# Late weight loads held on other filter rows, and the second batch's first stage started two steps later: a study of one change to a fused FFT-mixing and feed-forward kernel

## The chip, the cores and the metric

The kernel runs on one core of one Trainium2 chip. The metric is device time in microseconds (us) for one execution of the whole program.

A profile is one execution, recorded by the hardware. PE is TensorE (matmuls), PEld its weight loads, DVE is VectorE, ACT is ScalarE, POOL is GpSimd, SP is SyncE, which here only issues DMA transfers. "SPq" marks such an issue. Times in the profile count from the start of the span.

## The reference

Two stages, 8 batches of 3008 tokens of width 256.

```python
X = np.fft.rfft(x, axis=1)                       # x: (8, 3008, 256)
Y = X * (filt_r + 1j * filt_i)[None, :, :]       # filters: (1505, 256)
y = np.fft.irfft(Y, n=3008, axis=1)
h = y.reshape(-1, 256) @ w_in                    # w_in: (256, 2048)
g = h * (1 / (1 + np.exp(-beta * h)))
out = g @ w_out                                  # w_out: (2048, 256)
```

## The kernel before

The FFT is done as matmuls with small tables, in stages. Batch 0 is transformed first (about 35 us). Then the feed-forward part runs as 752 block steps, 16 to a block of 512 tokens, and the stages of the next batches are spread over these steps by a plan: `place(a, z, units)` spreads `units` over the steps `a` to `z`. One step is two matmuls of 512 columns with `win` (line 825), ACT's activation `gT`, and four matmuls of 256 columns with `wout` two steps later (line 860). All of it is in program order on each engine, so a unit of another batch that waits in PE's queue stops the block steps behind it: in the profile of before, step 2's matmuls stand behind a unit of line 619 that waited 1.75 us and start at 39.24 us.

The parts that matter here, cut:

```python
apool = pool("apool", 3)                     # three buffers for tiles with the tag "a1"
# ...
def load_filter(f_sb, filt, at, k0, n, eng): # "lo" rows: at..at+H; "hi" rows: at+H..at+M  (H = 32, M = 64)
    # ... returns [issue of the lo rows, issue of the hi rows]
for part in FG[1:]:                          # filter groups 1, 2, 3, on SyncE
    for h in (1, 0):                         # hi rows are issued first, then lo rows
        for f, at in ((filt_r, 0), (filt_i, M)):
            load_filter(fri, f, at, *part, nc.sync)[h]()
# ...
# The hold: GpSimd copies one element of a filter load, so it waits until that load has landed
# before it issues what stands behind in its own queue (profile of before: the hold ends at
# 23.1 us, the first win load is issued at 23.42 us).
held = setup.tile([P, 1], F32, name="held", tag="held")
for p0 in (0, M):
    gp.tensor_copy(held[p0 : p0 + H], fri[p0 : p0 + H, 3 * KG - 1, :1])
load_win(0); load_win(1); load_wout(0)
xs[1] = load_x(1, X_HALVES[:2])              # first half of batch 1's x
# ... some microseconds later, during batch 0's middle stages:
for h in range(1, 4):
    load_wout(h)
load_x(1, X_HALVES[2:], xs[1])               # second half of batch 1's x
mark3 = dpool.tile([1, D], BF16, name="mark3", tag="mark3")
nc.sync.dma_start(mark3[:], xs[1][:1, J - 1, :])   # a tiny transfer: holds SyncE until that half has landed (46.2 us)
# ... and behind it, still on SyncE:
for at in (0, M):
    for go in load_filter(frr, filt_r, at, 0, JG, nc.sync):   # four loads of 256 KB
        go()
zz0[0] = apool.tile([KP, JG, D], BF16, name="zz", tag="a1")   # batch 0 takes one of the three buffers
# ...
def s1(b, i, on_act):                        # stage 1: 16 units, a buffer "a1" for every 4 of them
    if jj == 0:
        s["a1"] = apool.tile([KP, JG, D], BF16, name="a1", tag="a1")
    ps = fpsum.tile([P, 512], F32, name="ps1", tag="f")
    nc.tensor.matmul(ps[:KP], lhsT=t1[:], rhs=s["x"][:, 2 * i : 2 * i + 2, :], start=True, stop=True)   # line 619
    evac(s["a1"][:, jj : jj + 2, :], ps[:KP], on_act)
    if jj + 2 == JG:
        nc.sync.dma_start(s["d1r"][:, g * JG : (g + 1) * JG, :], s["a1"][:])   # line 624: out to DRAM
# ...
    units = u1(1, True)                      # stage 1 of batch 1
    place(1, 7, units[: J // 4], per=2)
    at = place(9, 14, units[J // 4 :], per=2)
```

Of the kernel before, what the change touches and what calls it, by code (L numbers as in the profile page):

```python
# [24 lines left out]
M = 64  # L25
H = M // 2
NK = 24
J = 32
# [9 lines left out]
def kernel(  # L38
# [364 lines left out]


    held = setup.tile([P, 1], F32, name="held", tag="held")
    for p0 in (0, M):
        gp.tensor_copy(held[p0 : p0 + H], fri[p0 : p0 + H, 3 * KG - 1, :1])
    def load_win(h):
        fs = slice(h * FF // 2, (h + 1) * FF // 2)
# [216 lines left out]
    def a2_read(b):  # L626
        s = st[b]
        s["a2"] = []
        for h in range(NG):
            t = a2pool.tile([P, KG, D], BF16, name="a2", tag="a2")  # L630
            nc.sync.dma_start(t[:], s["d1c"][:, h * KG : (h + 1) * KG, :])
            s["a2"].append(t)
# [41 lines left out]
    def zz_read(b):  # L674
        s = st[b]
        s["zz"] = []
        for h in range(NJG):
            t = zzpool.tile([KP, JG, D], BF16, name="zz", tag="zz")
            nc.sync.dma_start(t[:], s["d2r"][:, h * JG : (h + 1) * JG, :])
            s["zz"].append(t)  # L680
# [15 lines left out]
    def place(a, z, units, clear=False, per=1):  # L696
        last_at = a
        for n, go in enumerate(units):
            at = a + (z - a) * n / max(1, len(units) - 1)
            at = max(int(at), last_at)  # L700
            if clear and (at % NFB < 2 or at % NFB > 13):
                at += (2 - at) % NFB
            while len(plan.get(at, ())) >= per:
                at += 1
            plan.setdefault(at, []).append(go)
            last_at = at
        return last_at

    def u1(b, act=False):
        def unit(i):  # L710
            def go():
                if i == 0:
                    start(b)
                s1(b, i, act and i % 2 == 1)

            return go

        return [unit(i) for i in range(J // 2)]

    def u23(b):  # L720
        return [lambda i=i: s23(b, i) for i in range(NK // 2 + VLAG)]

    def u4(b, act=False):
        return [lambda i=i: s4(b, i, act and i % 2 == 1) for i in range(J // 2)]
# [6 lines left out]
    def uf():  # L731
        return [
            go
            for k0 in range(JG, NK, JG)
            for at in (0, M)
            for go in load_filter(frr, filt_r, at, k0, JG, nc.sync)
        ]


    def ut(n):  # L740
        return [
            lambda k=k: nc.vector.tensor_scalar_mul(
                t3[M:P, k : k + NK // n], t3b[M:P, k : k + NK // n], -1.0
            )
            for k in range(0, NK, NK // n)
        ]
# [11 lines left out]
    first_step = [(S * b // TB) * NFB for b in range(B + 1)]  # L758
    if B > 1:
        units = u1(1, True)  # L760
        place(1, 7, units[: J // 4], per=2)
        at = place(9, 14, units[J // 4 :], per=2)
        place(at + 1, at + 1, [lambda: a2_read(1)] + uf(), per=9)
        place(14, 20, ut(4), per=2)
        at = place(25, 56, u23(1), per=2)
        assert at < 60
        place(60, 60, [lambda: zz_read(1)], per=9)
        place(67, 79, u4(1), per=2)
# [43 lines left out]
    for s in range(len(steps) + LAG):  # L812
# [28 lines left out]
        if s >= LAG:  # L841
# [16 lines left out]
            per = acc[0].shape[1]  # L858
# [48 lines left out]
```

## Time and profile before

792.9 us (median of 3 runs, 792.88 to 793.45). The profiled execution took 790.78 us, and its span is 788.9 us.

| quantity (profile of before) | value |
|---|---|
| PE busy | 777.6 us of 788.9 (99%) |
| largest PE wait on a DMA up to 100 us | 1.75 us, first half of batch 1's x |
| hold ends; first win load issued | 23.1 us; 23.4 us |
| second half of batch 1's x lets SyncE go on | 46.2 us |
| first stage-1 write issued | 48.3 us |

The head of the page gives the span and, for each engine, its busy time, share of the span and number of instructions.

```profile
span 788.9 us, 15550 instructions
...
PE 777.6 (99%) x6111; PEld 548.4 (70%) x6111; DVE 394.4 (50%) x645; ACT 597.0 (76%) x922; POOL 144.7 (18%) x143
```

PE is busy for 99%, so time can be won only where it idles or where its clock is reduced. The list of waits up to 100 us (engine, output and line, what it waited for; total us, times, longest) has these lines among others.

```profile
DVE a L109 <- DMA d<-a: 2.2, 1, 2.2
...
PE ps L619 <- DMA xg<-in_x_dram: 1.8, 1, 1.8
...
```

The second line is PE's wait for x.

PE's timeline around the wait (start, duration, engine, line, operation, output and inputs, shapes, count; in brackets the idle time before and what ended it):

```profile
35.87 1.03 PE L825 MATMUL hps<-y,win_sb 128*128 128x376 bf16 x6
38.66 0.78 PE L619 MATMUL ps<-xg,t 94*96 94x512 bf16 x2 [1.75 <-DMA xg<-in_x_dram]
39.24 1.06 PE L825 MATMUL hps<-y,win_sb 128*128 128x512 bf16 x2
```

The stages' table for the same time: stretch, its length, busy time of PE, PEld, DVE, ACT, POOL with the number of instructions, then the granted PE clock, the DMA engines' mean share and GB/s.

```profile
22.00:24.00 2.00, 1.68 (x24) 1.46 (x23) 2.00 (x6) 2.00 (x5) 1.17 (x3) 1.00 0.84 197
24.00:26.00 2.00, 2.00 (x34) 1.91 (x32) 2.00 (x4) 2.00 (x5) 2.00 (x4) 1.00 0.49 49
36.00:38.00 2.00, 0.91 (x6) 0.32 (x4) 0.37 (x2) 1.73 (x4) 0.86 (x1) 1.00 0.99 246
38.00:40.00 2.00, 1.34 (x4) 0.61 (x5) 0.69 (x1) 0.52 (x1) 0.00 (x0) 0.75 1.00 352
40.00:42.00 2.00, 2.00 (x13) 1.44 (x12) 0.75 (x2) 0.76 (x2) 1.47 (x1) 0.50 1.18 317
42.00:44.00 2.00, 2.00 (x14) 1.28 (x13) 0.54 (x1) 1.04 (x2) 2.00 (x2) 0.89 1.01 215
```

From 36 to 40 us PE is not full, and from 39 to 42.4 us its clock is granted at half (0.50 in the trace's record of the clock, for 3.413 us). At 24 to 26 us the DMA engines are half idle (share 0.49). GpSimd's timeline tells why: nothing is issued while it waits for the filter rows (3.79 and 0.34 us).

```profile
22.19 0.41 POOL L407 COPY held<-fri 32x1 f32<-32x1 f32 x1 [3.79 <-DMA fri<-in_filt_r_dram]
22.94 0.18 POOL L407 COPY held<-fri 32x1 f32<-32x1 f32 x1 [0.34 <-DMA fri<-in_filt_i_dram]
23.42 1.54 POOL L410 DMA_DIRECT2D win_sb<-in_moe_w_in_dram  x2 [0.30 <-issue]
```

SyncE's timeline shows when the second half of x has landed (the tiny transfer `mark<-xg` is issued in that moment), four filter loads behind it, and then the first stage-1 write. (That half comes in two transfers. The tiny one reads from the larger, which landed at 46.20 us; the smaller landed at 46.77 us.)

```profile
46.21 0.23 SPq L506 DMA_DIRECT2D mark<-xg  x1
46.48 0.31 SPq L131 DMA_DIRECT2D frr<-in_filt_r_dram  x1
...
48.33 6.05 SPq L624 DMA_DIRECT2D d<-a  x3
...
```

### The profile page before, as it was taken

Reading aid. Unit: us, or ns where it says so; the run is one execution under the profiler, and the core shown is the slowest. Engines: PE = TensorE matmul, PEld = TensorE weight load, DVE = VectorE, ACT = ScalarE, POOL = GpSimd, SP = SyncE. Lnnn points to the kernel's source line nnn. Section 1 sums busy time; section 2 is a strip of 40 time slices with the busy share of each in tenths; the row PEclk is TensorE's granted clock in tenths of the full one; section 3 lists DMA queues with packets and bytes.
Section 4 is the critical chain, followed back from the end, with each engine's and each line's share of the span. In section 5 each row is a group of like instructions: output and inputs, shape, how many; then the busy total and the mean of one; then the engine's idle time right before and its main releaser. Section 6 shows DMA issues by size and latency. Waiting matters only on the chain.

```text
span 788.9 us, 15550 instructions
## 1 busy us (share of the span) xinstructions
PE 777.6 (99%) x6111; PEld 548.4 (70%) x6111; DVE 394.4 (50%) x645; ACT 597.0 (76%) x922; POOL 144.7 (18%) x143
## 2 busy tenths in 40 slices
PE   8899999999999999999999999999999999999998
PEld 5767667766777667876668766687667766776665
DVE  8837935646537464465634746267452761500101
ACT  6877886886678866788677876778767788677776
POOL 8422500430013200131002310024000340000000
PEclk9999999999999999999999999999999999999999
DMA  9979674516901177012860228412370214110101
GB/s 192 219 190 230 163 202 140 126 67 187 228 33 60 55 212 208 28 67 94 195 177 28 95 97 191 152 54 77 115 211 27 75 67 127 45 37 28 54 27 54
DMA packets 84185, 91.46 MB, mean 116 GB/s; under 512 B 4498, under 2 KB 74276, under 8 KB 83154
## 3 DMA queue, kind: packets, MB, share of 16 engines
q1 hardware_dynamic: 81008, 73.95, 30.4%
q0 software_dynamic: 2816, 16.26, 10.6%
q8 instruction: 48, 0.79, 0.4%
q10 hardware_dynamic: 288, 0.26, 0.1%
q14 instruction: 25, 0.20, 0.1%
HBM read 57.16 MB, written 46.66 MB: 132 GB/s over the span
## 4 chain that ended last, share of the span: by engine, by line
PE 90%; DMA 6%; DVE 2%; issue 1%; POOL 1%; DVEq 0%; ACT 0%; SPq 0%; ACTq 0%; POOLq 0%
PE acc L860 40%; PE hps L825 39%; PE ps L619 3%; PE ps L544 2%; DMA xg<-in_x_dram 2%; PE ps L667 2%; PE ps L641 2%; DMA fri<-in_filt_i_dram 1%; DMA frr<-in_filt_r_dram 1%; DVE ost L109 1%; DMA out_dram<-ost 1%; DMA mark<-xg 1%; DVE q_t L656 0%; PE pz L536 0%; DVE q_t L653 0%
## 5 line engine op out<-in xcount | busy, mean ns | idle before, releaser
L834 ACT ACTIVATE gT<-hps,beta_sb 128x512 bf16<-128x512 f32 x752 | 516.1, 687 | 177.5 <-PE hps L825 166.4
L860 PE MATMUL acc<-wout_sb,gT 128*128 128x256 bf16 x3008 | 455.6, 272 | 1.2 <-ACT ost L107 0.2
L825 PE MATMUL hps<-y,win_sb 128*128 128x512 bf16 (+8 forms) x1730 | 448.3, 351 | 0.0
L860 PEld LDWEIGHTS <-gT 128*128 128x128 bf16 x3008 | 285.6, 98 | 132.8 <-issue 4.6
L825 PEld LDWEIGHTS <-win_sb 128*128 128x128 bf16 x1730 | 165.0, 98 | 24.5 <-issue 0.2
L657 POOL TENSOR_TENSOR v_t<-p_t,q_t 128x512 bf16<-128x512 f32 x84 | 106.7, 1270 | 393.4 <-DVE q_t L656 390.5
L109 DVE COPY ost<-acc 128x512 f32<-128x512 f32 (+1 forms) x88 | 56.2, 678 | 193.6 <-PE acc L860 190.6
L109 DVE CAST a<-ps 96x512 bf16<-96x512 f32 x96 | 65.9, 687 | 90.2 <-PE ps L619 87.9
L111 DVE TENSOR_SCALAR y<-ps 128x376 bf16<-128x376 f32 (+1 forms) x119 | 64.5, 545 | 62.6 <-PE ps L544 62.4
L652 DVE TENSOR_TENSOR p_t<-ps,frr 128x512 f32<-128x512 f32 x84 | 58.1, 692 | 32.0 <-PE ps L641 29.4
L656 DVE TENSOR_TENSOR q_t<-ps,fri 64x512 f32<-64x512 f32 x84 | 58.3, 694 | 1.2
L653 DVE SCALAR_TENSOR_TENSOR q_t<-ps,fri 64x512 f32<-64x512 f32 x84 | 57.4, 683 | 1.1
L544 PEld LDWEIGHTS <-zz 96*128 96x128 bf16 x512 | 35.3, 97 | 28.9
L107 ACT ACTIVATE z<-ps 128x512 bf16<-128x512 f32 x84 | 49.5, 589 | 0.8 <-PE ps L667 0.7
L619 PE MATMUL ps<-xg,t 94*96 94x512 bf16 x112 | 42.6, 385 | 1.8 <-DMA xg<-in_x_dram 1.8
L544 PE MATMUL ps<-t,zz 96*128 96x94 bf16 x448 | 36.7, 204 | 0.0
L667 PE MATMUL ps<-v_t,t 128*128 128x256 bf16 x168 | 32.1, 273 | 0.6 <-DVE q_t L656 0.6
L641 PE MATMUL ps<-a,t 128*128 128x256 bf16 x168 | 32.1, 273 | 0.0
L118 POOL DMA_DIRECT2D xg<-in_x_dram x22 | 12.1, 552 | 102.0 <-PE acc L860 97.8
L641 PEld LDWEIGHTS <-t 128*128 128x128 bf16 x168 | 15.8, 98 | 14.6
L619 PEld LDWEIGHTS <-t 94*96 94x96 bf16 x112 | 13.8, 124 | 14.1 <-DMA xg<-in_x_dram 2.2
L667 PEld LDWEIGHTS <-t 128*128 128x128 bf16 x168 | 15.4, 98 | 8.4 <-DVE q_t L656 1.4
(120 smaller groups left out, 196.8 us busy)
## 6 DMA issues: line engine op xcount, KB each, us to landing
out_dram<-ost SPq DMA_DIRECT2D x80, 256.0 KB, 2.1
d<-a SPq DMA_DIRECT2D x28, 384.0 KB, 3.8
a<-d SPq DMA_DIRECT2D x28, 384.0 KB, 5.3
d<-z SPq DMA_DIRECT2D x28, 384.0 KB, 2.3
zz<-d SPq DMA_DIRECT2D x28, 384.0 KB, 6.7
xg<-in_x_dram POOLq DMA_DIRECT2D x6, 1280.0 KB, 10.0
frr<-in_filt_r_dram SPq DMA_DIRECT2D x12, 256.0 KB, 7.4
out_dram<-ost SPq DMA_DIRECT2D x18, 128.0 KB, 2.7
```

The lines of the kernel that those rows point to most:

```text
L109: nc.vector.tensor_copy(dst, src)
L111: nc.vector.tensor_scalar_mul(dst, src, scale)
L544: nc.tensor.matmul(ps[:, e, :NP], lhsT=zz[:, jj + e, dc * P : (dc + 1) * P], rhs=tab[:], start=True, stop=True,)
L619: nc.tensor.matmul(ps[:KP], lhsT=t1[:], rhs=s["x"][:, 2 * i : 2 * i + 2, :], start=True, stop=True)
L641: nc.tensor.matmul(ps[:, e, :], lhsT=t2[:, k0 + e, 3:5, :].rearrange("p c k -> p (c k)"), rhs=s["a2"][g][:, kk + e, :], start=True, stop=True,
L652: nc.vector.tensor_tensor(p_t[:], ps[:], frr[:, ks_, :], ALU.mult)
L656: nc.vector.tensor_tensor(q_t[:M], ps[M:P], fri[M:P, ks_, :], ALU.mult)
L657: nc.gpsimd.tensor_tensor(v_t[:], p_t[:], q_t[:], ALU.add)
L667: nc.tensor.matmul(ps[:, e, :], lhsT=t3[:, k0 + e, :], rhs=v_t[:, e, :], start=True, stop=True)
L825: nc.tensor.matmul(hps[:, pos - t0 : pos - t0 + ln], lhsT=win_sb[:, dc, fb * P : (fb + 1) * P], rhs=ys[b][:, dc, n0 : n0 + ln], start=(dc ...
L834: nc.scalar.activation(gT[:, :tn], hps[:, :tn], ACT.Silu, scale=beta_sb[:, fb : fb + 1])
L860: nc.tensor.matmul(acc[tb // per][:, tb % per, :], lhsT=gT[:, tb * P : (tb + 1) * P], rhs=wout_sb[:, fb, :], start=(fb == 0 and tb % per = ...
```

## The change

Its intent is to let GpSimd issue the win, wout and x loads earlier, by waiting for rows of filter group 2 that are issued before the others and that landed before them: in the profile of before the hi rows' imaginary part landed at 21.36 us, and the waits for the lo rows ended at 22.19 and 22.94 us. A second edit, not in its short title, moves the first eight stage-1 units of batch 1 from steps 1 to 7 to steps 3 to 8, away from the landing of x. This is the whole diff.

```diff
     held = setup.tile([P, 1], F32, name="held", tag="held")
-    for p0 in (0, M):
+    for p0 in (H, M + H):
         gp.tensor_copy(held[p0 : p0 + H], fri[p0 : p0 + H, 3 * KG - 1, :1])
@@
         units = u1(1, True)
-        place(1, 7, units[: J // 4], per=2)
+        place(3, 8, units[: J // 4], per=2)
         at = place(9, 14, units[J // 4 :], per=2)
```

## The prediction

> **What bounds the kernel.** TensorE: the page gives PE 777.6 us busy of a 788.9 us span (99%); the chain of waits is 90% PE. Only PE idle time and reduced clock can be won. The list of waits up to 100 us has one large PE wait on a DMA: 1.75 us at line 619 (stage 1 of batch 1) for the first half of the second x. In the timeline PE ends block steps 0 and 1 at 36.9 us and starts line 619 at 38.66, when that half lands. Right behind it the stage table shows a granted clock of 0.75 (38 to 40 us), 0.50 (40 to 42), 0.79 (42 to 43), then 1.00; 512-column matmuls take 0.43 us there, elsewhere 0.22. [...] From 38.66 to 42.76 us PE did work that takes about 2.4 us at full clock: the dip costs about 1.7 us. Gap plus dip: 3.4 us.
>
> **What the change does.**
> 1. Hold: GpSimd waits for two filter loads before it issues the win, wout and x loads. A group's hi rows are issued before its lo rows. Before, the waits for the lo rows ended at 22.2 and 22.9 us, and the first win load was issued at 23.4. The hi rows of group 2 land near 21.4, so win should be issued near 22.0: 1.4 us earlier. The DMA share falls to 0.49 at 24 to 26 us. [...] filter group 3 may land some tenths later; DVE first reads it at 29.1 us, with slack. x half 1 should land near 37.2, half 2 near 45.4 instead of 46.8.
> 2. Placement (in the diff, not in its title): the first eight stage-1 units start at step 3, not 1. PE then first does step 2's matmuls, eight z transposes, step 0's output matmuls and step 3's matmuls (0.44 us each), and reaches line 619 near 38.8 us. That alone covers the old landing. Instruction counts stay equal.
>
> **On the critical path:** the whole gap and, following from it, the dip. A gap of 0.1 to 0.3 us may stay at step 2 (it needs ACT's first gT, done at 37.1). Next limits: wout part 1 is scaled by about 41 us, PE asks near 43; x half 2 is asked at about 46.4. The stretch with DVE 97% busy (70 to 90 us; PE gaps 0.27, 0.39, 0.24) should shift whole; I allow 0.3 us lost.
>
> **Predicted:** 792.9 - 3.4 + 0.3 = 789.8 us, range 787.6 to 791.8. Faster by over 2%: 0.01; within 2%: 0.98; slower by over 2%: 0.01.
>
> **Signs.** Right: win issued near 22.0 us; no PE wait on xg over 0.3 us; line 619 starts after 38 us without a gap; clock 1.00 from 36 to 44 us. Wrong: a wait on xg (half 2 too) or wout; hold end not earlier; the dip still there; later waits grown by what the start won.
>
> **What would make it wrong.** [...] absent in timed runs, the gain is about 1.7 us (791.2). [...] Waits at 60 to 90 us could eat the gain.

792.9 less 3.4 (1.75 of gap and an estimated 1.7 of dip, from the stage table and the matmul times of the profile of before) plus 0.3 is 789.8 us. That the dip follows from the gap was the estimate from one profile, in which half clock begins at 39.0 us, 0.4 us after the gap. "Absent in timed runs" is said of the dip.

## The result, and the profile after

The changed kernel took 789.45 us (median of 6 runs, 788.86 to 790.36) against 792.89 us before (6 runs, 790.48 to 794.96). The ratio is 0.996, with a 95% interval of 0.9941 to 0.9979. Ratios in this document are the mean time of one kernel's fast runs over the mean of the other's fast runs of the same rounds, so they are not quite the ratio of the medians quoted beside them. The result is correct.

So the predicted 789.8 us was met within 0.4 us. The profiles, though, do not show 3.4 us. The span is 787.6 us against 788.9: only 1.3 us.

```profile
span 787.6 us, 15550 instructions
...
PE 776.5 (99%) x6111; PEld 548.0 (70%) x6111; DVE 393.6 (50%) x645; ACT 597.0 (76%) x922; POOL 144.5 (18%) x143
```

The early part went as predicted. The hold ends at 21.6 us and the first win load is issued at 21.70 us instead of 23.42; the DMA engines are no longer idle at 24 to 26 us (share 1.03, was 0.49), and PE is full at full clock from 38 to 52 us.

```profile
20.71 0.18 POOL L407 COPY held<-fri 32x1 f32<-32x1 f32 x1 [2.40 <-DMA fri<-in_filt_r_dram]
21.46 0.18 POOL L407 COPY held<-fri 32x1 f32<-32x1 f32 x1 [0.57 <-DMA fri<-in_filt_i_dram]
21.70 1.55 POOL L410 DMA_DIRECT2D win_sb<-in_moe_w_in_dram  x2
```

```profile
24.00:26.00 2.00, 2.00 (x34) 1.90 (x32) 2.00 (x4) 2.00 (x4) 2.00 (x5) 1.00 1.03 186
36.00:38.00 2.00, 1.66 (x16) 0.98 (x15) 0.27 (x1) 1.85 (x5) 0.50 (x1) 1.00 1.06 356
38.00:40.00 2.00, 2.00 (x18) 1.36 (x16) 1.37 (x2) 1.37 (x3) 2.00 (x2) 1.00 1.09 305
40.00:42.00 2.00, 2.00 (x19) 1.43 (x18) 1.15 (x2) 0.96 (x3) 1.25 (x1) 1.00 1.01 207
52.00:54.00 2.00, 0.85 (x6) 0.41 (x5) 0.20 (x1) 0.22 (x1) 0.00 (x0) 1.00 1.15 346
54.00:56.00 2.00, 1.57 (x17) 1.19 (x17) 1.08 (x2) 2.00 (x5) 0.00 (x0) 1.00 0.43 129
```

But look at 52 to 56 us in this table: PE is busy for only 0.85 and 1.57 of 2 us. (In the profile before, PE was busy for 2.00 us in each of these two stretches.) The list of waits names the cause.

```profile
DVE a L109 <- DMA d<-a: 4.7, 1, 4.7
...
ACT a L107 <- DMA d<-a: 2.4, 1, 2.4
...
PE ps L544 <- ACT a L107: 1.6, 1, 1.6
```

DVE's wait for the write `d<-a` has grown from 2.2 to 4.7 us, ACT has one of 2.4 us that was not there, and PE waits 1.58 us for ACT. PE's and ACT's timelines show the same event:

```profile
54.43 0.33 PE L544 MATMUL ps<-t4b,zz 96*128 96x94 bf16 x4 [1.58 <-ACT a L107]
```

```profile
53.78 0.59 ACT L107 ACTIVATE a<-ps 96x512 bf16<-96x512 f32 x1 [2.37 <-DMA d<-a]
```

```profile
45.26 0.23 SPq L506 DMA_DIRECT2D mark<-xg  x1
...
47.37 9.34 SPq L624 DMA_DIRECT2D d<-a  x4
```

Stage 1 has three buffers, one of which batch 0 holds first. The fourth group of four units takes the buffer of the first group, so it must wait until that group's write to DRAM has landed. The write stands in SyncE's queue behind the tiny transfer that waits for the second half of x (45.26 us, was 46.21) and behind four filter loads; it is issued at 47.37 us (was 48.33). I call this the second gate. The first gate is the wait for the first half of x near 38 us. In the profile before, PE reached the second gate late (the same transforms of line 544 at 55.90 us) and found it open:

```profile
55.90 0.33 PE L544 MATMUL ps<-t4b,zz 96*128 96x94 bf16 x4
```

By the traces' records of landings the write had landed at 54.30 us before and at 53.68 us after. In the profile after PE came early and went on at 54.43 us, 0.75 us behind the landing. With the same 0.75 us the gate of the profile before was open at about 55.05 us (an estimate from these records), so PE came only 0.85 us late there. The bookkeeping of the two profiles closes: 1.75 us of gap and about 1.7 us of half clock were removed, 1.58 us and another 0.34 us (step 2 waits for ACT's first gT at 37.15 us, which the prediction had expected) were added, and 1.75 + 1.7 - 1.58 - 0.34 is 1.5, near the 55.90 - 54.43 = 1.47 us that PE is ahead. Seen from the gate, the same 1.47 us are the 0.85 us by which PE had been late and the 0.62 us by which the write landed earlier.

That explains the profiles but not the 3.4 us of the timed runs. The experiments had to settle that.

### The profile page after: what moved, and what is told of

It is laid out like the page before. It is cut to its first block, busy times and chain, and to the rows that moved or that the text cites. A ratio compares the mean times of both kernels' runs of the same rounds, so it can differ in the third digit from the quotient of the medians.

```text
span 787.6 us, 15550 instructions
## 1 busy us (share of the span) xinstructions
PE 776.5 (99%) x6111; PEld 548.0 (70%) x6111; DVE 393.6 (50%) x645; ACT 597.0 (76%) x922; POOL 144.5 (18%) x143
## 4 chain that ended last, share of the span: by engine, by line
PE 93%; DVE 4%; issue 2%; DMA 1%; ACT 1%; DVEq 0%; ACTq 0%
PE acc L860 41%; PE hps L825 40%; PE ps L619 3%; PE ps L544 3%; PE ps L641 2%; PE ps L667 2%; PE pw L187 1%; DVE ost L109 1%; DMA d<-a 1%; DVE qb_t L444 1%; DVE pb_t L444 0%; DVE q_t L656 0%; ACT gT L834 0%; DVE q_t L653 0%; PE psa L325 0%
## 5 line engine op out<-in xcount | busy, mean ns | idle before, releaser
L109 DVE COPY ost<-acc 128x512 f32<-128x512 f32 (+1 forms) x88 | 56.3, 678 | 193.8 <-PE acc L860 190.6
```

Of the source, the lines that this page charges most:

```text
L109: nc.vector.tensor_copy(dst, src)
```

## The experiments

Main theory (two gates): what counts is when the first stage-1 write lands; the first gate's gap is mostly hidden behind that. Then the hold wins the time, because it moves the second half of x, and the placement wins nothing. Rival: the first gap and its half clock are the gain, as predicted, and either half of the change could remove it. Runs of one group shared a chip and the runs of the kernel before.

| run | hold | placement | SyncE's order | median us (before on that chip) | ratio, 95% interval | PE gaps over 0.3 us, 36 to 60 us |
|---|---|---|---|---|---|---|
| c_after | hi | new | old | 789.18 (793.2) | 0.9953, 0.9939 to 0.9967 | 0.35, 1.14 |
| c_hold | hi | old | old | 789.73 (793.2) | 0.9958, 0.9944 to 0.9971 | 2.44 |
| c_place | lo | new | old | 792.96 (793.2) | 1.0, 0.9987 to 1.0013 | 0.34, 0.73, 2.46 |
| c_early | hi | new | write first | 787.56 (793.2) | 0.9935, 0.9921 to 0.9949 | 0.34 |
| d_before_early | lo | old | write first | 789.8 (791.9) | 0.997, 0.9958 to 0.9982 | 1.63, 0.46 |
| d_hold_early | hi | old | write first | 787.36 (791.9) | 0.9943, 0.993 to 0.9956 | none |
| d_place_early | lo | new | write first | 788.61 (791.9) | 0.9963, 0.9949 to 0.9976 | 0.34, 1.74 |
| d_fill | lo | old, gap filled | old | 791.44 (791.9) | 0.9996, 0.9984 to 1.0008 | 2.43 |
| e_mark_first | hi | new | mark, write, loads | 787.8 (792.76) | 0.9941, 0.9925 to 0.9957 | 0.34 |
| e_hold_g1 | hi of group 1 | new | old | 789.13 (792.76) | 0.9955, 0.9937 to 0.9973 | 0.34, 1.60 |

All ten gave correct results. The gaps are read from each run's PE timeline.

The kept traces settle what the gate decides. From this group of line 544 to the end of the span it takes 733.0 to 733.1 us in eleven of the twelve profiles (both kernels and the ten runs); in c_place it takes 734.6 us, with a half-clock stretch behind the gate. In the six profiles in which PE waits at the gate (after, c_after, c_hold, c_place, d_fill, e_hold_g1), line 544 starts 0.75 us after the first write has landed. So in these six the span is the landing plus 0.75 plus about 733.0 us, and 1.7 us more in c_place; what PE lost before the gate does not enter. With the hold on the hi rows of group 2 the write landed at 53.2 to 54.8 us (after, c_after, c_hold), with the lo rows at 54.3, 55.9 and 56.3 us (before, c_place, d_fill).

### The changed kernel again

No edit against the changed kernel.

> The changed kernel again, beside its halves on one chip. Main theory (two gates): the early gap on x (1.75 us) and its half-clock stretch vanish, but stage 1 of batch 1 then runs into a second gate, the first write of stage 1's results to DRAM, which stands in SyncE's queue behind a small transfer that waits for the second half of x; so a PE gap of about 1.6 us stands near 54 us and the profile shows about 1.3 us won against the profile of before. Expected here: the same new gap of 1 to 2 us before line 544 near step 14, half clock nowhere between 36 and 60 us, time 2 to 4 us below before. Rival (no second gate): no gap over 0.5 us there; the gap seen once was chance.

Measured: 789.18 us, and the gap is there again, 1.14 us before line 544 at 53.98 us, with full clock from 36 to 60 us. The rival that the gap was chance is out.

### The hold alone

```diff
-    for p0 in (0, M):
+    for p0 in (H, M + H):
```

> The hold on the hi rows alone, stage-1 units at step 1 as before. The first half of x lands near 36.1 us, before PE asks at 36.9, so the gap on x is under 0.2 us and the clock stays full. Two-gates theory: the second half of x lands about 1 us earlier than before as in the changed kernel, so PE runs into the same gate near 54 us with a gap of 1 to 2 us; time within 0.6 us of the changed kernel. Rival (placement carries the gain): time stays within 0.6 us of before.

Measured: 789.73 us, 0.5 us above the changed kernel and 3.5 us below before in the medians. There is no gap on x at 37 us, because its first half has already landed. At the second gate PE waits 2.44 us, more than the 1 to 2 us expected:

```profile
55.52 0.33 PE L544 MATMUL ps<-t4b,zz 96*128 96x94 bf16 x4 [2.44 <-ACT a L107]
```

It does not arrive earlier than in the profile of the changed kernel (53.08 us against 52.85), but the write lands later (54.77 us against 53.68). This profile is of one of the run's slower executions, 790.37 us. The intervals of hold alone and of the whole change overlap: the hold is the change, as far as time can tell.

### The placement alone

```diff
-        place(1, 7, units[: J // 4], per=2)
+        place(3, 8, units[: J // 4], per=2)
```

> The placement alone, the hold on the lo rows as before. PE reaches line 619 near 38.8 us, just as the first half of x lands (38.6), so no early gap over 0.3 us and no half clock. Two-gates theory: the second half of x lands near 46.5 us as before, so the gate near 54 us stands about 0.8 us later than in the changed kernel: PE gap there (or at the second half of x, near step 9) of 2 to 3 us in sum, profile span 0.5 to 1 us above the changed kernel's. Rival (placement carries the gain, the hold nothing): span and time equal to the changed kernel's within 0.3 us.

Measured: 792.96 us, a ratio of 1.0. The placement does what it was made for, since the first gap shrinks from 1.75 to 0.73 us, and it wins nothing. The reduced clock does not hide a gain: all six runs were at 0.997 to 0.998, and their mean, 792.99 us, is 0.4 us below the eight runs of before on that chip at such a clock (793.4). PE's timeline shows where the time went:

```profile
39.77 0.63 PE L619 MATMUL ps<-xg,t 94*96 94x512 bf16 x2 [0.73 <-DMA xg<-in_x_dram]
...
47.95 0.39 PE L619 MATMUL ps<-xg,t 94*96 94x512 bf16 x1 [0.23 <-DMA xg<-in_x_dram]
...
56.62 0.33 PE L544 MATMUL ps<-t4b,zz 96*128 96x94 bf16 x4 [2.46 <-ACT a L107]
```

SyncE passed the second half of x at 47.23 us, 2.5 us later than in c_after (44.78), and the write left at 49.34 us.

```profile
47.23 0.23 SPq L506 DMA_DIRECT2D mark<-xg  x1
...
49.34 3.19 SPq L624 DMA_DIRECT2D d<-a  x3
```

My expected size was wrong: I had allowed 0.5 to 1 us to the changed kernel, and the span is 791.26 against 786.94 us. Of these 4.3 us, 2.64 are the later gate (56.62 against 53.98 us at line 544). The rest is a half-clock stretch of 3.4 us that follows the gap at the gate and is paid in full (an estimate from the granted clocks below, 0.98, 0.50 and 0.67); half of 3.4 is 1.7 and the sum is 4.3.

```profile
54.00:56.00 2.00, 0.16 (x1) 0.00 (x0) 0.00 (x1) 0.02 (x1) 0.00 (x0) 1.00 1.15 347
56.00:58.00 2.00, 1.38 (x13) 1.00 (x13) 1.28 (x2) 2.00 (x5) 0.00 (x0) 0.98 0.48 145
58.00:60.00 2.00, 2.00 (x14) 1.48 (x14) 1.04 (x2) 1.15 (x3) 0.00 (x0) 0.50 0.25 71
60.00:62.00 2.00, 1.78 (x13) 1.26 (x12) 0.01 (x1) 0.71 (x2) 0.00 (x0) 0.67 0.45 125
```

### The first write ahead in SyncE's queue

On top of the changed kernel, the tiny transfer and the four filter loads are issued at block step 7, behind the first stage-1 write.

```diff
-                mark3 = dpool.tile([1, D], BF16, name="mark3", tag="mark3")
-                nc.sync.dma_start(mark3[:], xs[1][:1, J - 1, :])
...
-    for at in (0, M):
-        for go in load_filter(frr, filt_r, at, 0, JG, nc.sync):
-            go()
...
         place(3, 8, units[: J // 4], per=2)
+        def late_frr():
+            mark3 = dpool.tile([1, D], BF16, name="mark3", tag="mark3")
+            nc.sync.dma_start(mark3[:], st[1]["x"][:1, J - 1, :])
+            for p in (0, M):
+                for go in load_filter(frr, filt_r, p, 0, JG, nc.sync):
+                    go()
+
+        place(7, 7, [late_frr], per=9)
```

> The changed kernel with the first stage-1 write put ahead of the small waiting transfer and of the four filter loads in SyncE's queue (these are issued at step 7 instead of before the blocks). Two-gates theory: the write lands near 47 us instead of 53.7, ACT and DVE no longer wait for it, the PE gap near 54 us is gone, time about 1.5 us below the changed kernel. Rival (the gap is caused by something else, such as DMA bandwidth or ACT's load): a gap over 1 us stays between 50 and 60 us and the time is that of the changed kernel within 0.4 us.

Measured: 787.56 us, 1.6 us below the changed kernel on the same chip. The write is issued at 43.17 us (the trace has no record of its landing), and neither DVE nor ACT nor PE waits for `d<-a` any more; the only PE gap left between 36 and 60 us is the 0.34 us at step 2.

```profile
43.17 0.32 SPq L618 DMA_DIRECT2D d<-a  x1
44.30 0.23 SPq L758 DMA_DIRECT2D mark<-xg  x1
...
46.82 7.98 SPq L618 DMA_DIRECT2D d<-a  x3
```

The second gate is therefore the write's place in SyncE's queue; the work of ACT and PE is the same here. Whether the wait on x or the four loads held it is asked below.

### The same order with the parts of the change taken away

The same edit on the kernel before, on the hold alone and on the placement alone. Where the units start at step 1, the loads are issued at step 6, so that they stand between the first and the second write as in c_early. Against c_early, the three differ by these lines (d_before_early has both, d_hold_early the second alone, d_place_early the first alone):

```diff
-    for p0 in (H, M + H):
+    for p0 in (0, M):
...
-        place(3, 8, units[: J // 4], per=2)
-        place(7, 7, [late_frr], per=9)
+        place(1, 7, units[: J // 4], per=2)
+        place(6, 6, [late_frr], per=9)
```

> The kernel before with only SyncE's first stage-1 write put ahead of the waiting transfer and the filter loads: the second gate is taken away, the first stays. Two-gates theory: the gap on the first half of x (1.7 us or more) and the half clock after it are now paid in full, so the time is about 3.4 us above the early-write version with hold and placement, that is about 791 us; with no half clock about 789.5. Rival (the first gate never mattered, the second alone sets the time): about 787.6, as the early-write version.

> Hold on the hi rows plus early write, stage-1 units at step 1. Two-gates theory: the first half of x lands before PE asks, the second gate is gone: time within 0.4 us of the early-write version with both (787.6), no PE gap over 0.5 us between 36 and 60 us. Rival (the placement is needed as well): about 1 us or more above it with a gap on x.

> Placement plus early write, hold on the lo rows as before. Two-gates theory: gap on the first half of x up to 0.7 us, on the second half of x (near step 9) up to about 1 us, second gate gone: 788 to 789.5 us, far below the placement without early write (793.0), which shows that the placement did remove the first gap and lost the gain at the second gate. Rival (the placement costs something of its own): stays above 791.

Measured: 789.8, 787.36 and 788.61 us. Without the second gate the first one is seen: the kernel before then keeps a gap of 1.63 us on the first half of x and one of 0.46 us on the second half, and it lies 2.4 us above the version with the hold. No half clock followed in its profile, and its five runs show a granted clock of 0.999 to 1.0, so the lower of my two figures (789.5) was the right one. The placement's 0.6 us against the kernel with early write alone (means 788.99 and 789.59) is not clear of the noise: the intervals overlap, and the two profiles have the same span, 787.6 us. The gap on the first half of x is gone, but PE meets the second half:

```profile
48.51 0.39 PE L613 MATMUL ps<-xg,t 94*96 94x512 bf16 x1 [1.74 <-DMA xg<-in_x_dram]
```

With the hold, neither half of x is waited for, and the placement adds nothing: 787.36 us without it, 787.56 with it (on another chip).

### The first gap filled with idle matmuls

```diff
         units = u1(1, True)
+        stage1 = units[0]
+
+        def filled():
+            wt = fpsum.tile([P, TB], F32, name="wt", tag="f")
+            for _ in range(8):
+                nc.tensor.matmul(
+                    wt[:], lhsT=t3[:, 0, :], rhs=win_sb[:, 0, :TB], start=True, stop=True
+                )
+            stage1()
+
+        units[0] = filled
```

> The kernel before with eight idle 512-column matmuls (1.7 us of work, result unused) in the gap in which PE waits for the first half of x, so that no half clock can follow it. Two-gates theory: the time won by the full clock after 38.7 us is spent at the second gate, near 54 us: a PE gap of 1 to 2 us appears there and the time is within 0.7 us of before. Rival (the first gap and its half clock are what the change wins): about 1.7 us below before.

Measured: 791.44 us, ratio 0.9996. There is no gap and no half clock near 38 us, and at the second gate PE waits 2.43 us. All five runs show full clock (1.0). They average 791.6 us.

```profile
57.09 0.33 PE L544 MATMUL ps<-t4b,zz 96*128 96x94 bf16 x4 [2.43 <-ACT a L107]
```

Idle matmuls do not bring x earlier: stage 1 starts at 38.93 us here and at 38.66 in the profile of before. So this run takes away the half clock behind the gap and not the gap's delay. It shows that the full clock gains nothing there, since the write landed only at 56.34 us; for the gap itself the evidence is c_place.

This is to be read beside the kernel before itself, whose 33 timed runs in the three groups come with their clocks: 12 with a mean granted clock of 0.999 or more average 791.4 us (790.5 to 792.1), the other 21, at 0.996 to 0.998, average 793.2 us (791.9 to 795.0). One stretch of 3.4 us at half clock lowers the mean over the span by 0.002 (the profile of before, with one such stretch, has 0.998), so by this estimate these are runs with one or two such stretches. A before-run without a dip (a half-clock stretch) thus costs what the filled kernel costs, and a lower clock goes with 1.8 us more in 21 of 33 runs.

Such a dip need not be the one behind the first gap. In the profile of before, gap and dip together (3.45 us) made PE only 0.85 us late at the gate. With the write landing as in d_fill (56.34 us) the gate lets PE go at 57.09 us, 1.2 us after the 55.90 us at which PE came in spite of gap and dip; both would then cost nothing. A dip behind the second gate costs all of its 1.7 us, as in c_place (734.6 us from the gate to the end, 733.0 to 733.1 in the others). So the dips that the timed runs of before paid for were probably there; this is an estimate from the profiles and is not shown.

### Which of the two blockers in SyncE's queue

The changed kernel with only the four filter loads moved behind the write; the tiny transfer keeps its place.

```diff
-    for at in (0, M):
-        for go in load_filter(frr, filt_r, at, 0, JG, nc.sync):
-            go()
...
+        def late_frr():
+            for p in (0, M):
+                for go in load_filter(frr, filt_r, p, 0, JG, nc.sync):
+                    go()
+
+        place(7, 7, [late_frr], per=9)
```

> The changed kernel with the four filter loads moved behind the first stage-1 write in SyncE's queue, but the small transfer that waits for the second half of x still ahead of it. Two blockers stood ahead of the write: that wait (to about 45.3 us) and then four loads of 256 KB. Theory A (the loads ahead of the write cost the time): the write is issued near 45.5 us and lands before group 4 of stage 1 asks for its buffer near 51 us; no PE gap over 0.5 us between 50 and 60 us, time about 787.6 as in the early-write version. Theory B (the wait on x is enough): a gap near 54 us stays, time near 789.

Measured: 787.8 us, no gap near 54 us. The write leaves at 44.71 us, right behind the tiny transfer, and it lands at 48.17 us by the trace's record, 3.5 us later; behind the four loads it had taken from 47.37 to 53.68 us, 6.3 us. So the wait on x was bearable, and the 1 MB of loads ahead of the write was what delayed it, in its issue (46.89 us in c_after) and in its landing.

### The hold on still earlier rows

```diff
-        gp.tensor_copy(held[p0 : p0 + H], fri[p0 : p0 + H, 3 * KG - 1, :1])
+        gp.tensor_copy(held[p0 : p0 + H], fri[p0 : p0 + H, 2 * KG - 1, :1])
```

> The changed kernel with the hold on the hi rows of filter group 1 instead of group 2 (in the trace of before the imaginary part of these landed at 16.6 us), so the weight loads are issued near 18.5 us instead of 21.7 to 22.0. Theory A (the gain of the hold came from filling the hole in the DMA engines' work at 23 to 26 us, which the change has closed already): the second half of x lands at most 0.7 us earlier, the gap near 54 us shrinks by no more than that or filter loads come late for DVE, time within 0.7 us of the changed kernel (789.2). Theory B (each us of earlier issue is a us at the second gate): the second half of x lands about 3 us earlier, the gap is gone, time near 787.6.

Measured: 789.13 us, near the changed kernel on two other chips (789.18 and 789.45). The weight loads are issued at 18.71 us, 3.0 us earlier than in the changed kernel, and in the profile the second half of x is not earlier at all: SyncE passes it at 46.18 us (45.26 there). The six runs spread from 787.4 to 790.63 us and the profile is of one of the slower, 790.28 us, so the usual landing may be somewhat earlier.

```profile
18.35 0.42 POOL L407 COPY held<-fri 32x1 f32<-32x1 f32 x2
18.71 1.54 POOL L410 DMA_DIRECT2D win_sb<-in_moe_w_in_dram  x2
```

```profile
46.18 0.23 SPq L506 DMA_DIRECT2D mark<-xg  x1
```

The change had already filled the hole in the DMA engines' work (0.49 to 1.03 at 24 to 26 us). From 18 to 36 us their share is 0.98 before, 1.06 in the changed kernel and 1.08 here, so in these profiles the earlier issue moved hardly more. By my estimate it mostly reordered the transfers: the weight loads were issued 3.0 us earlier, and the first half of x was complete at 37.12 us, 36.12 in the changed kernel.

## Why the prediction was right, point by point

- **The time and the range: right.** 789.45 us against 789.8.
- **The hold, 1.4 us earlier: right, a little small.** The first win load moved from 23.42 to 21.70 us, 1.7 us. The profile before had the earliest issue of the five profiles with the lo rows; the others have 23.7 to 23.9 us.
- **The hole in the DMA work leaves room: right.** It was filled (share 0.49 to 1.03 at 24 to 26 us), and in e_hold_g1 no more was to be had in the median: weight loads issued 3.0 us earlier from GpSimd's queue won nothing, and in its profile other transfers came later (the first half of x was complete at 37.12 us, 36.12 in the changed kernel). The reason given for a later filter group 3 was not shown, and a delay of tenths is not seen: the one transfer of the group with a recorded landing, the imaginary part of its hi rows, landed at 24.61 us before and 24.65 us after.
- **"x half 1 should land near 37.2, half 2 near 45.4 instead of 46.8": the right direction, sizes off.** By the trace's records of landings the first half was complete at 36.1 us and the second at 45.9. SyncE passed the second half at 45.26 us instead of 46.21, 0.95 us earlier, not 1.4. For the usual run of before the shift is larger, because the other four profiles with the lo rows have this at 47.2 to 47.8 us; the profile I predicted from was a quick one.
- **The placement "alone covers the old landing": half right, and without worth.** In c_place the first half of x was complete later than in the profile before (39.73 us, was 38.62), and 0.73 us of gap stayed. The time did not move.
- **"On the critical path: the whole gap and, following from it, the dip": wrong.** This is the step that failed, together with "should shift whole; I allow 0.3 us lost". Most of gap and dip was hidden behind the second gate: of 3.45 us they cost about 0.85 us in the profile of before, by the estimate above. Taking away 1 us of the gap won nothing (c_place, ratio 1.0), and taking away the dip won nothing clear of noise (d_fill, 0.9996). What set the time where PE waits at the gate is the landing of the first write (plus 0.75 and about 733.0 us), and the hold moved that landing. The wait of DVE on `d<-a` (2.2 us, no PE wait with it) was already in the list of waits. I read it as harmless since PE did not wait, and did not ask what would happen when PE came 3 us earlier.
- **"Absent in timed runs, the gain is about 1.7 us": right as far as it goes.** The size of the dip, 1.7 us, fits: before-runs with and without a lower clock (0.996 to 0.998 in 21 runs, 0.999 or more in 12) differ by 1.8 us. That their dip is the one behind the first gap is not shown, nor is what decides whether a run has one.
- **Sign "later waits grown by what the start won": it came true in part**, with 1.58 us.

The predicted sum, 1.75 of gap and 1.7 of dip, less 0.3, is 3.1 us. The measured sum has other terms. The means of the undipped before-runs and of c_after are 791.4 and 789.25: 2.2 us, which the hold won at the second gate. A dip of 1.8 us in 21 of 33 runs adds 1.2 us on average. 2.2 + 1.2 is 3.4 us. This split is by the listed clocks; it is supported by c_hold (all of the gain, undipped), c_place (none of it, its six runs at 0.997 to 0.998) and d_fill (undipped, no other gain). The two sums agree, but they are not the same sum; that the time was met within 0.4 us is in good part luck. Had only the placement been made, the same argument would have promised over 3 us and won nothing.

What stays open: whether the dips in the timed runs of before follow the first gap, as in its profile, or the second, as in c_place's, which the landings make the likelier. Their lists give the clock of a whole run only, and of the kernel before there is only one profile.

The best kernel here is the changed one with the first write put ahead in SyncE's queue (c_early 787.56, e_mark_first 787.8 us, and d_hold_early 787.36 us, which keeps the old placement): about 5 us below before and 1.6 us below the change.

## What to carry to other kernels

When a stall is to be removed, look for the next one in the same stretch first: a wait on another engine that has no wait of the bottleneck beside it (here DVE's 2.2 us on `d<-a`) can be a gate that the bottleneck has just been too late to meet (here by 0.85 us, as estimated above). Shrinking the first stall (c_place) or its half clock (d_fill) and leaving the gate won nothing, and moving the gate won 2.4 us in the means even where the stall stayed (d_before_early). A cheap test is to measure, in each profile, the time from a point behind the gate to the end: where it is the same everywhere (733.0 us here), only the gate's opening counts. Filling a stall with idle work tests the clock alone, since the work behind it starts no earlier (38.93 us in d_fill, 38.66 in the profile of before). And put a write that frees a buffer ahead of bulk loads that nobody needs soon: order in an issuing queue, not the amount of traffic, decided 1.6 us here (c_early against c_after).

## What the traces showed of the clock and of SyncE's queue

- A half-clock stretch followed PE gaps of 1.75 us (before) and 2.46 us (c_place); in the profile of before it lasted 3.413 us. None followed in the profiles with a gap of 1.74 us (d_place_early), 1.63 (d_before_early), 1.60 (e_hold_g1), 1.58 (after), 1.14 (c_after), 2.43 (d_fill) or 2.44 us (c_hold): their granted clock over the whole run is 0.999 to 1.0, where before and c_place, with one stretch each, have 0.998. So the length of a gap alone did not decide it, and what did is not shown.
- The 33 runs of the kernel before split by their clock into 791.4 us (12 runs, 0.999 or more) and 793.2 us (21 runs, 0.996 to 0.998), wider than the effects under study, so the clock of each run must be read before small differences are.
- In the profile after, SyncE's tiny transfer is issued at 45.26 us, as soon as the larger transfer of x has landed (45.24 us), and everything behind it later. What that did to the write behind: it could be issued at 43.17 us (c_early) and was issued at 46.89 us (c_after), behind one waiting transfer and four loads, and PE waited 1.14 us for it.
